# A dilated causal convolution with a gated output on one core: staging copies and input loads tied to TensorE's place in the plan, other DMA durations in the planner, and two items of a unit exchanged

## The chip, the cores and the metric

The kernel runs on one core of a Trainium2 chip. The metric is device time in microseconds (us), the median over runs of the same program. The kernel before took 342.98 us (median of 3 runs, 342.66 to 343.67).

## What is computed

`x` is 2 x 16000 x 144, `w` is 15 x 144 x 288 and `w_o` is 144 x 144, all bf16. Every time step gets the sum over 15 taps, two steps apart and looking back, of a row of `x` times a 144 x 288 matrix; the two halves of the 288 results go through tanh and sigmoid, are multiplied, and the product is projected by `w_o`:

```python
xp = jnp.pad(x, ((0, 0), (pad, 0), (0, 0)))
h = jnp.einsum('btc,cd->btd', xp[:, pad:pad + T, :], w[0])
for i in range(1, K):
    off = pad - i * dil
    h = h + jnp.einsum('btc,cd->btd', xp[:, off:off + T, :], w[i])
f = h[..., :D].copy()
g = h[..., D:].copy()
z = jnp.tanh(f) * _sigmoid(g)
return z @ w_o
```

## The kernel before

**Tiling.** The 32000 time steps are cut into 128 segments of 250, one for each partition. Step `e` of all segments together is one tile: 128 segments by 144 channels. TensorE needs the channels on the partitions, so each tile is transposed. Eight steps are an *octet* `o` (0 to 30), two octets are a *pair* `m` (octets 2m+1 and 2m+2). The 144 channels are split: 128 of them go into the tiles `XA`, the other 16, of eight taps side by side, into the tiles `XB`.

**Staging of a pair.** A load brings 16 steps into `Xr` (two buffers; L476). For each octet VectorE copies the 128 channels into the contiguous buffer `STA` (L634), and a DMA transpose turns that into `XA` (L636). VectorE also packs the 16 channels into `XBc` (`compact_chunk`, L533); ScalarE copies from there, in two halves per octet, into `STB` (L653), and a DMA transpose makes `XB` of it (L655). `STA` and `STB` have two buffers each, so a copy must wait until the transpose of the octet before the last has landed. `XA` has 11 slots, `XB` 7. The function `stage(m)` adds all this to the plan for a pair. `prepare(m)` adds VectorE's differences of such tiles (L672: `V`, `DU`, `DD`, `BE`, `BF`, and `GX`, `GU`, `GV`, `GD` for a pair).

**The arithmetic of a unit.** The 15 taps are not run as 15 products per step: sums of weights (`WC`, `WS`, `WT`, `WV`, `WD`) and differences of tiles give eight outputs with fewer products. A *unit* is one parity of a pair and makes eight output steps; there are 30. Its items, in the order of the string `PATTERN`, are groups of matmuls of 128x128 weights with 288 columns (L726). `S0`, `X0a`, `X1a` and `Y0a` each run two matmuls into one bank of a pair of PSUM banks, and ScalarE copies the bank to its neighbour (L890); `S1`, `X0b`, `X1b`, `Y0b` then add to both. ScalarE moves `X` results to `UX` (L959) and `S1`'s to a second pair (L917). VectorE combines: `VE`'s and `VF`'s results plus `UX` (L1011, three per unit, into the memory of `Xp`; L1032, one), and these plus `Y` (L1023, three). The last items `D11`, `D00`, `D10`, `D01` end in tanh and sigmoid on ScalarE (L747, L750; `TS`) and a product on VectorE (L755; `Z`). A DMA transposes `Z` to `ZT` (L814), TensorE multiplies by `w_o` (L831), ScalarE copies the result to `OS` (L839), and a DMA stores it (L850). In the string, a `+` means that the item belongs to the unit after the current one; `O` marks a place for a group of `w_o` matmuls.

**The order of the work.** Nothing of this order is written out for the other engines. Each operation is added to a graph with its reads, writes, a duration and a priority, and a list scheduler (`_Graph.run`) plays the program with those durations: each engine takes the operation that can start first, TensorE's main items in the order in which they were added. What comes out is a fixed sequence for each of TensorE, ScalarE, VectorE, GpSimd and SyncE (which issues nearly all DMAs). On the chip, each engine runs its sequence strictly in order; waits are semaphores of true dependencies. The argument `soft` names operations whose planned start must come first; it shapes the sequence and is no wait on the chip. Before, `prepare`'s steps are spread over two units, twelve per pair, each `soft` on TensorE's latest operation at that place (the list `gate`); `stage`'s operations are added at once for the whole pair and carry no `soft`, so the scheduler puts them as early as buffers and engines allow. A DMA's planned end is its issue, plus its bytes at 280 GB/s, one DMA after the other, plus `DMA_LAT` (2.3 us).

Of the kernel before, what the change touches and what calls it, by code (L numbers as in the profile page):

```python
# [9 lines left out]
F32 = mybir.dt.float32  # L10

NP = 128
DMA_LAT = 2.3
DMA_RATE = 280e3
MM = 0.1227
TAIL = {"pe": 0.165, "act": 0.095, "dve": 0.088, "pool": 0.1, "sp": 0.0}
# [56 lines left out]
class _Graph:  # L73
# [58 lines left out]
    def run(self, hint):  # L132
# [18 lines left out]
        dma_free = 0.0  # L151
# [40 lines left out]
        while n < len(self.ops):  # L192
# [34 lines left out]
            free[op.eng] = st + op.dur  # L227
            if op.dma:
                t0 = max(dma_free, st + op.dur)
                dma_free = t0 + op.nbytes / DMA_RATE  # L230
                op.end = dma_free + DMA_LAT
            else:
                op.end = st + op.dur + TAIL[op.eng]
            ai[0] += 1 if op.alloc and not op.floating else 0
# [93 lines left out]
def _conv_wavenet_kernel(nc, x, w, w_o, out):  # L328
# [19 lines left out]
    NPAIR = NOCT // 2  # L348
# [7 lines left out]
    NX = 2  # L356
# [11 lines left out]
    KF = 6  # L368
    LAG = 2
    SPREAD = 12  # L370
    PATTERN = "Y0a O2+ X0a+ O1+ Y0b X0b+ D11 D00 X1a+ S0+ D10 Y01 S1+ X1b+ D01 VE+ O0+ VF+"

    with contextlib.ExitStack() as st:
        def sb(name, shape, dt):
# [38 lines left out]

        g = _Graph()

        XpF = Xp[:].rearrange("p e d -> p (e d)").bitcast(F32)

        def bank(b):
# [211 lines left out]
        def load_xa(o):  # L630
            s, q = aslot(o), o % NST
            ci = chunk_of(8 * o)
            i0 = 8 * o - CH[ci][0]
            g.add("dve", lambda v: v.tensor_copy(STA[:, q, :, :], Xr[:, ci % NX, i0:i0 + 8, 0:DA]),  # L634
                  r=[("Xr", ci % NX)], w=[("STA", q)], dur=0.335, prio=2)
            g.add("sp", lambda e: e.dma_start_transpose(XA[:, s, :, :], STA[:, q, :, :].rearrange("p a b -> p (a b)")),  # L636
                  r=[("STA", q)], w=[("XA", s)], dur=1.3, dma="xa", nbytes=8 * 128 * 128 * 2)

        def load_xb(o):
            s, q = bslot(o), o % NST  # L640
            e0 = E0 + 8 * o
            ck = set()
            for e in range(e0 - 28, e0 + 8):
                if e >= EP:
                    ck.add(("XBc", chunk_of(e - E0)))
                else:
                    ck.update(hk5 + ["XBcz"])
            m4 = (e0 + 2) // 4

            for h in range(2):  # L650
                def cp(v, h=h):
                    src = bass.AP(XBc[:].tensor, (MB - 1 - m4 - h) * DB, [[4 * MB * DB, NP], [MB * DB, 4], [1, 128]])
                    return v.activation(STB[:, q, 4 * h:4 * h + 4, :], src, ACT.Copy)  # L653
                g.add("act", cp, r=sorted(ck, key=str), w=[("STB", q, h)], dur=0.5, prio=2)
            g.add("sp", lambda e: e.dma_start_transpose(XB[:, s, :, :], STB[:, q, :, :].rearrange("p a b -> p (a b)")),  # L655
                  r=[("STB", q, 0), ("STB", q, 1)], w=[("XB", s)], dur=1.3, dma="xb", nbytes=8 * 128 * 128 * 2)

# [1 line left out]
            return [("XB", bslot(o))]  # L659

        TR = 128
        gate = []

        def ap(t, off, dims):
            full = t[:].tensor
# [487 lines left out]
            b_diffs(o)  # L1153

        def stage(m):

            if m >= NPAIR:
                return
            for o in (2 * m + 1, 2 * m + 2):
                fetch(o)  # L1160
                if o > 2:
                    load_xa(o)
                    while nd[0] < len(CH) and CH[nd[0]][0] <= 8 * o:
                        compact_chunk(nd[0])
                        nd[0] += 1
                    load_xb(o)

        def prepare(m):
            o0, o1 = 2 * m + 1, 2 * m + 2
# [13 lines left out]
        reach = max(o for _, o in pattern)  # L1183
        todo = [(-1, 2, 1), (0, 0, 2), (0, 1, 2), (0, 2, 2)]
        done_d = {}
        stage(1)
        for f in prepare(0):
            f()
        todo_p = []
        for t in range(-reach, NUN):  # L1190
            if t % 2 and t >= -1:
                stage((t + 1) // 2 + 2)
                todo_p = prepare((t + 3) // 2)
                step = 0
            for name, off in pattern:
                while todo_p and step * SPREAD >= (12 - len(todo_p)) * 2 * len(pattern):
                    gate[:] = [op for op in g.ops[-40:] if op.eng == "pe"][-1:]
                    todo_p.pop(0)()
                    gate[:] = []
                step += 1  # L1200
                if name[0] == "O":
                    for _ in range(2 if t >= NUN - 3 else 1):
                        if t >= 0 and todo and todo[0][2] <= t:
                            project(*todo.pop(0)[:2])
                    continue
                u = t + off
                if not 0 <= u < NUN:
                    continue
                if name[0] == "G":
                    if (u, int(name[1]), int(name[2])) in late:  # L1210
                        late.pop((u, int(name[1]), int(name[2])))()
                    continue
                ITEMS[name](u)
                if name[0] == "D":
                    done_d[u] = done_d.get(u, 0) + 1
                    m, r, o0, o1 = octs(u)
                    if done_d[u] == 4 and r == 1 and u < NUN - 1:
                        for o in (o0, o1):
                            ship(o, range(8))
                            todo += [(o, gi, t + LAG) for gi in range(3)]  # L1220
                    elif done_d[u] == 4 and u == NUN - 2:
                        for o in (o0, o1):
                            ship(o, (0, 2, 4, 6))
# [98 lines left out]
```

## Time and profile before

| what | value |
|---|---|
| time, median of 3 runs | 342.98 us |
| the profiled execution's own time | 342.79 us |
| its span, first to last instruction | 340.8 us |
| mean granted TensorE clock | 0.997 |
| TensorE matmul busy | 327.4 us (96%) |
| VectorE busy | 303.3 us (89%) |
| ScalarE busy | 258.8 us (76%) |
| GpSimd busy | 17.5 us (5%) |

The profile is of one execution. Engines are called PE (matmul), PEld (weight load, beside PE), DVE (VectorE), ACT (ScalarE), POOL (GpSimd) and SP (SyncE; SPq is its queue). A row of the timeline gives the start of a run of like instructions from the span's start, how long it lasted, engine, line, operation, tiles written and read, shape and count; in brackets stands the engine's idle time ahead of it and what ended it. A matmul's recorded end is modelled and lies beyond the start of the next one. Rows of the stage table give, for each stretch, each engine's busy time with its count of instructions, the granted clock and the DMA engines' busy share.

### The profile page before, as it was taken

The page shows a single profiled execution, that of the slowest core. Times are in us where ns is not written, and L with a number is a line of the kernel's source. Part 1 is how long each engine was busy: PE and PEld are TensorE (multiplying, and loading weights), DVE is VectorE, ACT ScalarE, POOL GpSimd, SP SyncE. Part 2 cuts the span into 40 slices and gives each one's busy share as a digit, 9 for nine tenths or more (in the row PEclk, how much of TensorE's full clock was granted, in tenths as well). Part 3 has the DMA queues.
Part 4 walks back from the last instruction along what each step waited for, and adds up shares of the span by engine and source line. Part 5 has one row for each costly group of instructions (what it writes and reads, how often), then busy time and mean ns, then how long its engine had stood idle before and what let it go on. Part 6 is the DMA issues. An engine that isn't in the chain of part 4 may idle for free.

```text
span 340.8 us, 7123 instructions
## 1 busy us (share of the span) xinstructions
PE 327.4 (96%) x2736; PEld 246.3 (72%) x2736; DVE 303.3 (89%) x662; ACT 258.8 (76%) x626; POOL 17.5 (5%) x30
## 2 busy tenths in 40 slices
PE   7899899799999999999999999999999999999996
PEld 6777576476777777777777777777777777777773
DVE  2999889799989999999999999998998989895672
ACT  3238477888888978788797878888887777778764
POOL 8650000000000000000000000000000000000000
PEclk9999999999999999999999999999999999999998
DMA  8789999877657495965957496570654261231453
GB/s 214 252 133 212 237 224 197 184 160 169 120 145 151 113 188 116 203 132 143 129 144 141 109 202 132 101 148 19 145 86 105 67 87 54 61 79 37 104 106 104
DMA packets 112509, 46.46 MB, mean 136 GB/s; under 512 B 103822, under 2 KB 106303, under 8 KB 112477
## 3 DMA queue, kind: packets, MB, share of 16 engines
q1 hardware_dynamic: 111961, 45.68, 63.1%
q8 instruction: 21, 0.34, 0.4%
q0 software_dynamic: 512, 0.33, 0.4%
q14 instruction: 11, 0.09, 0.1%
q10 hardware_dynamic: 4, 0.01, 0.0%
HBM read 11.82 MB, written 9.22 MB: 62 GB/s over the span
## 4 chain that ended last, share of the span: by engine, by line
PE 80%; DMA 8%; ACT 5%; DVE 5%; issue 1%; SPq 1%
PE PS L726 70%; PE PS L831 7%; DMA XB<-STB 6%; ACT STB L653 2%; DMA Xp<-in_x_dram 1%; DVE Xp L1011 1%; ACT UX L959 1%; ACT TS L747 1%; ACT TS L750 1%; DVE PS L1023 1%; DVE WC L614 1%; ACT PS L890 0%; DVE Z L755 0%; SPq L476 0%; PE PS L781 0%
## 5 line engine op out<-in xcount | busy, mean ns | idle before, releaser
L1011 DVE TENSOR_TENSOR Xp<-PS,UX 128x576 f32<-128x576 f32 x90 | 65.2, 752 | 13.8 <-PE PS L726 13.0
L1023 DVE TENSOR_TENSOR PS<-PS,Xp 128x576 f32<-128x576 f32 x90 | 68.4, 760 | 2.7 <-PE PS L726 1.1
L726 PE MATMUL PS<-WA,GD 128*128 128x288 bf16 x360 | 69.9, 286 | 0.3 <-DVE PS L1023 0.3
L890 ACT ACTIVATE PS<-PS 128x288 f32<-128x288 f32 x120 | 45.7, 406 | 22.7 <-PE PS L726 22.7
L747 ACT ACTIVATE TS<-PS 128x288 f16<-128x288 f32 x125 | 51.8, 414 | 11.1 <-PE PS L726 9.0
L750 ACT ACTIVATE TS<-PS 128x288 f16<-128x288 f32 x125 | 51.6, 413 | 0.0
L959 ACT ACTIVATE UX<-PS 128x576 f32<-128x576 f32 x60 | 39.0, 650 | 15.9 <-PE PS L726 13.7
L653 ACT ACTIVATE STB<-XBc 128x512 bf16<-128x512 bf16 x60 | 36.3, 633 | 16.3 <-DMA XB<-STB 11.3
L726 PE MATMUL PS<-WS,GU 128*128 128x288 bf16 x210 | 44.1, 286 | 0.0
L839 ACT ACTIVATE OS<-PS 128x432 bf16<-128x432 f32 (+1 forms) x88 | 42.4, 488 | 0.8
L755 DVE TENSOR_TENSOR Z<-TS 128x288 bf16<-128x288 f16 x125 | 37.6, 301 | 5.9 <-ACT TS L750 5.7
L831 PE MATMUL PS<-WOR,ZT 128*128 128x144 bf16 (+1 forms) x322 | 42.3, 253 | 0.2 <-ACT TS L750 0.2
L726 PEld LDWEIGHTS PS<-WA,GD 128*128 128x128 bf16 x360 | 34.6, 98 | 10.5 <-DVE PS L1023 1.9
L726 PE MATMUL PS<-WB,XB 128*128 128x288 bf16 x140 | 37.6, 286 | 0.0
L726 PE MATMUL PS<-WB,BF 128*128 128x288 bf16 x120 | 34.3, 286 | 0.0
L726 PE MATMUL PS<-WB,BE 128*128 128x288 bf16 x120 | 34.3, 286 | 0.0
L831 PEld LDWEIGHTS PS<-WOR,ZT 128*128 128x128 bf16 x322 | 27.9, 98 | 6.7 <-ACT OS L839 0.6
L726 PE MATMUL PS<-WD,DD 128*128 128x288 bf16 x180 | 31.9, 286 | 0.2 <-ACT PS L890 0.2
L726 PE MATMUL PS<-WA,DD 128*128 128x288 bf16 x180 | 30.8, 287 | 0.1
L726 PE MATMUL PS<-WC,V 128*128 128x288 bf16 x180 | 30.6, 286 | 0.0
L726 PE MATMUL PS<-WT,DU 128*128 128x288 bf16 x120 | 24.8, 288 | 2.4 <-DVE Xp L1011 1.6
L726 PEld LDWEIGHTS PS<-WS,GU 128*128 128x128 bf16 x210 | 20.3, 98 | 5.7 <-ACT PS L890 0.4
(89 smaller groups left out, 517.7 us busy)
## 6 DMA issues: line engine op xcount, KB each, us to landing
Xr<-in_x_dram SPq DMA_DIRECT2D x15, 576.0 KB, 4.0
out_dram<-OS SPq DMA_DIRECT2D x29, 288.0 KB, 2.4
WA<-in_w_dram SPq DMA_DIRECT2D x3, 288.0 KB, 5.7
ZT<-Z SPq DMA_TRANSPOSE x32, 3.6
Xp<-in_x_dram SPq DMA_DIRECT2D x2, 252.0 KB, 5.7
XA<-STA SPq DMA_TRANSPOSE x30, 3.4
XB<-STB SPq DMA_TRANSPOSE x30, 3.3
Xp<-in_x_dram SPq DMA_DIRECT2D x1, 441.0 KB, 3.7
```

The costliest lines, as they stand in the source:

```text
L614: g.add(eng, lambda v: v.tensor_tensor(dst(), a(), b(), ALU.add), r=r, w=wk, dur=dur)
L653: return v.activation(STB[:, q, 4 * h:4 * h + 4, :], src, ACT.Copy)
L726: return lambda t: t.matmul(bank(bk.b), lhsT=lhs(), rhs=rhs(), start=start, stop=True, skip_group_check=True)
L747: return a.activation(TS[:, s, 0, :, :], both(bk, 0, D), ACT.Tanh)
L750: return a.activation(TS[:, s, 1, :, :], both(bk, D, D), ACT.Sigmoid)
L755: return v.tensor_tensor(dst, TS[:, s, 0, :, :], TS[:, s, 1, :, :], ALU.mult)
L831: return t.matmul(PS[:, c0:c0 + n * D], lhsT=ZT[:, zt, blk, :], rhs=WOR[:, wi:wi + n, :].rearrange("p a b -> p (a b)"), start=first, stop= ...
L839: return e.tensor_copy(dst, src) if eng == "dve" else e.activation(dst, src, ACT.Copy)
L890: g.add("act", lambda e: e.activation(bank(bk.b + 1), bank(bk.b), ACT.Copy), w=[bk], dur=t_act(N2), prio=0)
L959: g.add("act", lambda e: e.activation(UX[:, k, u % NU, :, :], both(X, 0, N2), ACT.Copy), r=[X], w=[("UX", k, u % NU)], frees=[X], dur=t_ac ...
L1011: g.add("dve", lambda v, k=k, wi=wi, vb=vb, us=us: v.tensor_tensor(wslot(wi), both(vb, 0, N2), UX[:, k, us, :, :], ALU.add), r=[vb, ("UX", ...
L1023: return v.tensor_tensor(both(d, 0, N2), src, wslot(wi), ALU.add)
```

## The change

Three things. First, `stage` no longer adds a pair's staging at once: it returns seven steps (two loads, the packing, two `XA` octets, two `XB` octets), which the main loop releases at even distances over part of two units (`SPREAS`), and the copies into `STA` and `STB` carry `soft` on the TensorE operation that was added last before them. `gate` is now set once for each place of the pattern, from main items alone. Second, the planner's DMA model: a transpose moves its bytes at 168 GB/s and then takes 0.6 us, the first loads of `x` and the weights keep 2.3 us, every other DMA takes 1.3 us after its bytes. Third, `S0` and `X1a` change places in `PATTERN`.

```diff
             if op.dma:
                 t0 = max(dma_free, st + op.dur)
-                dma_free = t0 + op.nbytes / DMA_RATE
-                op.end = dma_free + DMA_LAT
+                turn = op.dma in ("xa", "xb", "zt")
+                dma_free = t0 + op.nbytes / (DMA_RATE * (0.6 if turn else 1.0))
+                op.end = dma_free + (0.6 if turn else 2.3 if op.dma in ("xp", "wa", "wb") else 1.3)
...
-    PATTERN = "Y0a O2+ X0a+ O1+ Y0b X0b+ D11 D00 X1a+ S0+ D10 Y01 S1+ X1b+ D01 VE+ O0+ VF+"
+    SPREAS = 10
+    PATTERN = "Y0a O2+ X0a+ O1+ Y0b X0b+ D11 D00 S0+ X1a+ D10 Y01 S1+ X1b+ D01 VE+ O0+ VF+"
...
-                  r=[("Xr", ci % NX)], w=[("STA", q)], dur=0.335, prio=2)
+                  r=[("Xr", ci % NX)], w=[("STA", q)], dur=0.335, prio=2, soft=gate[:1])
...
-                g.add("act", cp, r=sorted(ck, key=str), w=[("STB", q, h)], dur=0.5, prio=2)
+                g.add("act", cp, r=sorted(ck, key=str), w=[("STB", q, h)], dur=0.5, prio=2, soft=gate[:1])
...
         def stage(m):
-
             if m >= NPAIR:
-                return
-            for o in (2 * m + 1, 2 * m + 2):
-                fetch(o)
-                if o > 2:
-                    load_xa(o)
-                    while nd[0] < len(CH) and CH[nd[0]][0] <= 8 * o:
-                        compact_chunk(nd[0])
-                        nd[0] += 1
-                    load_xb(o)
+                return []
+            o0, o1 = 2 * m + 1, 2 * m + 2
+
+            def pack():
+                while nd[0] < len(CH) and CH[nd[0]][0] <= 8 * o1:
+                    compact_chunk(nd[0])
+                    nd[0] += 1
+            return [lambda: fetch(o0), lambda: fetch(o1), pack, lambda: load_xa(o0), lambda: load_xa(o1), lambda: load_xb(o0), lambda: load_xb(o1)]
...
             if t % 2 and t >= -1:
-                stage((t + 1) // 2 + 2)
-                todo_p = prepare((t + 3) // 2)
+                todo_p, n_p, todo_s, n_s = prepare((t + 3) // 2), 12, stage((t + 5) // 2), 7
                 step = 0
             for name, off in pattern:
-                while todo_p and step * SPREAD >= (12 - len(todo_p)) * 2 * len(pattern):
-                    gate[:] = [op for op in g.ops[-40:] if op.eng == "pe"][-1:]
+                gate[:] = [op for op in g.ops[-60:] if op.eng == "pe" and not op.floating][-1:]
+                while todo_p and step * SPREAD >= (n_p - len(todo_p)) * 2 * len(pattern):
                     todo_p.pop(0)()
-                    gate[:] = []
+                while todo_s and step * SPREAS >= (n_s - len(todo_s)) * 2 * len(pattern):
+                    todo_s.pop(0)()
+                gate[:] = []
```

The sequences of the engines that come out differ as follows; after the change the line numbers are one or two higher (L653 becomes L655, L634 L636, L890 L891, L1011 L1012).

ScalarE near the start, from the copies for octet 4 on, before: `STB` rows are the staging copies, `UX` and `PS<-PS` belong to unit 0, `TS` is tanh and sigmoid.

```order
L653 ACTIVATE STB<-XBc 128x512 x2
L959 ACTIVATE UX<-PS 128x576
L890 ACTIVATE PS<-PS 128x288 x2
L653 ACTIVATE STB<-XBc 128x512 x2
L959 ACTIVATE UX<-PS 128x576
L917 ACTIVATE PS<-PS 128x2x288
L653 ACTIVATE STB<-XBc 128x512 x4
L747 ACTIVATE TS<-PS 128x288
L750 ACTIVATE TS<-PS 128x288
L890 ACTIVATE PS<-PS 128x288 x2
```

The same place after:

```order
L655 ACTIVATE STB<-XBc 128x512 x2
L960 ACTIVATE UX<-PS 128x576
L891 ACTIVATE PS<-PS 128x288 x2
L960 ACTIVATE UX<-PS 128x576
L918 ACTIVATE PS<-PS 128x2x288
L655 ACTIVATE STB<-XBc 128x512 x2
L891 ACTIVATE PS<-PS 128x288
L748 ACTIVATE TS<-PS 128x288
L751 ACTIVATE TS<-PS 128x288
L655 ACTIVATE STB<-XBc 128x512
L891 ACTIVATE PS<-PS 128x288
L655 ACTIVATE STB<-XBc 128x512
```

Before, the copies of octets 5, 6 and 7 stand ahead of this tanh; after, only octet 5's do, octet 6's stand behind it, and octet 7's come some thirty instructions later.

ScalarE in the middle of the run, around the start of a unit that has staging, before:

```order
L839 ACTIVATE OS<-PS 128x432
L653 ACTIVATE STB<-XBc 128x512 x2
L959 ACTIVATE UX<-PS 128x576
L653 ACTIVATE STB<-XBc 128x512
L747 ACTIVATE TS<-PS 128x288
L750 ACTIVATE TS<-PS 128x288
L747 ACTIVATE TS<-PS 128x288
L750 ACTIVATE TS<-PS 128x288
L890 ACTIVATE PS<-PS 128x288 x2
L653 ACTIVATE STB<-XBc 128x512
```

After, the four copies of a pair stand here:

```order
L748 ACTIVATE TS<-PS 128x288
L751 ACTIVATE TS<-PS 128x288
L655 ACTIVATE STB<-XBc 128x512
L840 ACTIVATE OS<-PS 128x288
L655 ACTIVATE STB<-XBc 128x512
L891 ACTIVATE PS<-PS 128x288
L840 ACTIVATE OS<-PS 128x432
L891 ACTIVATE PS<-PS 128x288
L840 ACTIVATE OS<-PS 128x432
L655 ACTIVATE STB<-XBc 128x512 x2
L960 ACTIVATE UX<-PS 128x576
```

All four moved ahead of the `UX` copy of `X0b`; none is left among the tanh and sigmoid rows of the unit.

VectorE in the middle of the run, the second half of a unit with staging, before:

```order
L672 TENSOR_TENSOR V<-XA 128x1024
L672 TENSOR_TENSOR DU<-XA 128x512
L755 TENSOR_TENSOR Z<-TS 128x2x144
L634 COPY STA<-Xr 128x1024 x2
L755 TENSOR_TENSOR Z<-TS 128x2x144
L672 TENSOR_TENSOR GX<-XA 128x512
L1023 TENSOR_TENSOR PS<-PS,Xp 128x2x288
L755 TENSOR_TENSOR Z<-TS 128x2x144
L672 TENSOR_TENSOR GU<-DU 128x1024
L1011 TENSOR_TENSOR Xp<-PS,UX 128x576
```

After:

```order
L535 COPY XBc<-Xr 128x4x4x16
L673 TENSOR_TENSOR V<-XA 128x1024
L756 TENSOR_TENSOR Z<-TS 128x2x144
L673 TENSOR_TENSOR DU<-XA 128x512
L756 TENSOR_TENSOR Z<-TS 128x2x144
L636 COPY STA<-Xr 128x1024
L1024 TENSOR_TENSOR PS<-PS,Xp 128x2x288
L756 TENSOR_TENSOR Z<-TS 128x2x144
L673 TENSOR_TENSOR GX<-XA 128x512
L673 TENSOR_TENSOR GU<-DU 128x1024
L636 COPY STA<-Xr 128x1024
L1012 TENSOR_TENSOR Xp<-PS,UX 128x576
```

The two `STA` copies of a pair stand apart, the second directly ahead of the first combine of the next `VE`; the packing into `XBc` is in this unit, where before it stood in the other. TensorE's main items keep their order but for the exchange of `S0` (`WT,XA`) and `X1a` (`WT,DU`).

6 lines of the change are left out of this document (3 added, 3 removed).

## The prediction

> **What bounds the kernel now.** I read the page, then busy time in three stretches, cut where `S1` starts in unit 0 (31.76 us), unit 3 (68.78) and unit 27 (301.64). The first holds three units and the rest of the direct products for the first outputs, the second 24 units, the third the end.
>
> ```profile
> span 340.8 us, 7123 instructions
> PE 327.4 (96%) x2736; PEld 246.3 (72%) x2736; DVE 303.3 (89%) x662; ACT 258.8 (76%) x626; POOL 17.5 (5%) x30
> ...
> PE 80%; DMA 8%; ACT 5%; DVE 5%; issue 1%; SPq 1%
> ```
> ```profile
> 31.76:68.78 37.02, 32.39 (x255) 23.28 (x252) 32.50 (x74) 26.15 (x63) 0.00 (x0) 1.00 0.97 203
> 68.78:301.64 232.86, 231.62 (x1897) 173.26 (x1897) 221.74 (x473) 192.37 (x471) 0.00 (x0) 1.00 0.61 125
> 301.64:340.80 39.16, 35.62 (x294) 26.12 (x293) 23.96 (x49) 26.33 (x66) 0.00 (x0) 0.97 0.34 84
> ```
>
> TensorE is on the chain that ended last for 80% of the span, and busy for 96%. Its rows in the first stretch, and in two units of the second, give its pace and its waits.
>
> ```profile
> 25.76 1.63 PE L726 MATMUL PS<-WB,XB 128*128 128x288 bf16 x12
> 27.23 0.41 PE L726 MATMUL PS<-WT,DU 128*128 128x288 bf16 x2
> ...
> 39.21 0.42 PE L726 MATMUL PS<-WV,V 128*128 128x288 bf16 x2 [0.92 <-DVE Xp L1011]
> ...
> 41.34 0.42 PE L726 MATMUL PS<-WT,DU 128*128 128x288 bf16 x2 [0.73 <-ACT TS L750]
> ...
> 44.96 0.42 PE L726 MATMUL PS<-WA,GD 128*128 128x288 bf16 x2 [0.32 <-DVE PS L1023]
> ...
> 51.79 0.42 PE L726 MATMUL PS<-WT,DU 128*128 128x288 bf16 x2 [0.42 <-DVE Xp L1011]
> ...
> 61.27 0.42 PE L726 MATMUL PS<-WV,V 128*128 128x288 bf16 x2 [0.89 <-ACT UX L959]
> 61.87 0.55 PE L831 MATMUL PS<-WOR,ZT 128*128 128x144 bf16 x4 [0.18 <-ACT TS L750]
> 63.54 0.42 PE L726 MATMUL PS<-WT,DU 128*128 128x288 bf16 x2 [1.13 <-DVE Xp L1011]
> ```
> ```profile
> 199.99 0.53 PE L831 MATMUL PS<-WOR,ZT 128*128 128x144 bf16 x4
> 200.36 0.65 PE L726 MATMUL PS<-WD,DD 128*128 128x288 bf16 x4
> ...
> 204.52 0.41 PE L726 MATMUL PS<-WD,DD 128*128 128x288 bf16 x2
> 204.87 0.66 PE L726 MATMUL PS<-WC,GX 128*128 128x288 bf16 x4
> ...
> 208.80 0.53 PE L831 MATMUL PS<-WOR,ZT 128*128 128x144 bf16 x4
> 209.35 0.42 PE L726 MATMUL PS<-WT,DU 128*128 128x288 bf16 x2
> ...
> 213.02 0.41 PE L726 MATMUL PS<-WT,DU 128*128 128x288 bf16 x2
> 213.46 0.42 PE L726 MATMUL PS<-WT,XA 128*128 128x288 bf16 x2
> ```
>
> Twelve matmuls of 288 columns go from 25.76 to 27.23: one every 0.1225 us. Two last 0.41, so the recorded end lies 0.16 us beyond the point where the next could start: a wait in brackets is 0.16 longer for TensorE, and one under 0.16 isn't shown. A unit has 68 such matmuls (8.33 us) and three `w_o` groups, two of four (0.37 each, 199.99 to 200.36) and one of three (0.25: a matmul of 288 columns less). That is 9.32 us without a wait. The second stretch takes 232.86/24 = 9.70 per unit: 0.38 lost in each, 9.1 us in all. In the first stretch there are 252 matmuls, 11 of them in `w_o` groups: 241 x 0.1225 + 0.99 = 30.5, so 6.5 us are lost. DVE's busy time in the second stretch, 221.74 or 9.24 per unit, is the next bound, right under TensorE's 9.32.
>
> **The first stretch, term by term.** ScalarE here, and one row of VectorE:
>
> ```profile
> 33.87 0.64 ACT L917 ACTIVATE PS<-PS 128x576 f32<-128x576 f32 x1
> 37.10 1.15 ACT L653 ACTIVATE STB<-XBc 128x512 bf16<-128x512 bf16 x2 [2.59 <-DMA XB<-STB]
> 39.54 1.15 ACT L653 ACTIVATE STB<-XBc 128x512 bf16<-128x512 bf16 x2 [1.29 <-DMA XB<-STB]
> 40.60 0.39 ACT L747 ACTIVATE TS<-PS 128x288 f16<-128x288 f32 x1
> ...
> 60.04 0.63 ACT L653 ACTIVATE STB<-XBc 128x512 bf16<-128x512 bf16 x1 [1.93 <-DMA XB<-STB]
> ```
> ```profile
> 36.06 0.23 DVE L533 COPY XBc<-Xr 128x256 bf16<-128x256 bf16 x1 [1.09 <-DMA Xr<-in_x_dram]
> ```
>
> Staging copies placed too early sit at the head of ScalarE's queue and wait for the transpose that still reads their buffer; tanh, sigmoid and `UX` copies behind them wait too, and TensorE waits for these. After the change octet 6's copies stand behind the tanh of 40.60 and octet 7's far later. So:
> - 41.34 (0.73 + 0.16 = 0.89) goes; what is late next is octet 6's copy, but the transpose that it needs landed at 37.10 even now.
> - 61.27, 61.87 and 63.54 (0.89 + 0.18 + 1.13 + 3 x 0.16 = 2.68) follow from the copy at 60.04. They go, but for about 0.06 at `X0a`: 2.6.
> - 51.79 (0.58): no copy of DVE's into `STA` stands ahead of this combine any more. The rest of the chain stays; I take 0.2.
> - 39.21 (0.92 + 0.16 = 1.08): DVE's first combine stood behind the packing that waited 1.09 for its load; now the packing stands behind two combines, and one `STA` copy between them. I take half, 0.5; the bounds are 0 and 1.08.
> - 44.96 (0.48) waits for a bank and stays.
>
> Sum 4.2, and about 0.3 for three waits at `S1` (next part): 4.5. Bounds: 3.0 (39.21 and 51.79 stay, 41.34 halves) and 5.3 (all but 44.96 and the rest of 51.79).
>
> **The second stretch.** Three waits of a unit matter. At `S1` (`WC,GX`, 204.87) the two matmuls before it would have let it start at 204.77: 0.10, since ScalarE copies `X1a`'s bank first and `S0`'s second. With `S0` first, its copy runs first, earlier by the other copy (0.40 long, as at 228.51), and the 0.10 goes; `X1a`'s copy is wanted only after `S1`, 0.49 later. At 209.35 `X0a` should have started at 209.17 (0.18), at 213.46 `S0` at 213.26 (0.20): both in the unit with staging, where ScalarE's sequence is this:
>
> ```profile
> 222.27 0.41 ACT L747 ACTIVATE TS<-PS 128x288 f16<-128x288 f32 x1 [0.43 <-PE PS L726]
> ...
> 226.85 0.41 ACT L750 ACTIVATE TS<-PS 128x288 f16<-128x288 f32 x1
> 227.28 0.41 ACT L839 ACTIVATE OS<-PS 128x288 bf16<-128x288 f32 x1
> 228.51 0.40 ACT L890 ACTIVATE PS<-PS 128x288 f32<-128x288 f32 x1 [0.81 <-PE PS L726]
> ...
> 231.33 0.62 ACT L653 ACTIVATE STB<-XBc 128x512 bf16<-128x512 bf16 x1
> 231.86 0.41 ACT L747 ACTIVATE TS<-PS 128x288 f16<-128x288 f32 x1
> ```
>
> A copy holds ScalarE for 0.53 (231.33 to 231.86), a tanh row for 0.3. Ahead of a tanh it delays the release of the bank that `S0` takes: the 0.20. After the change no copy stands there. Two stand between 227.16 (end of the sigmoid row) and the `L890` copy at 228.51: 1.35 us, into which 2 x 0.53 and the `OS` copy's 0.3 just fit. The other two go ahead of `UX`, which comes some 0.3 late; 0.43 of idle time before the next tanh hides that. If a copy costs 0.1 more than here, `X0a`'s copy is late and `X0b` waits about 0.2 per pair.
>
> DVE keeps its amount of work. The best units now, near the end, where nothing is staged:
>
> ```profile
> 282.55 0.66 PE L726 MATMUL PS<-WC,GX 128*128 128x288 bf16 x4
> ...
> 292.05 0.42 PE L726 MATMUL PS<-WC,GX 128*128 128x288 bf16 x2
> ```
>
> 9.50, with the 0.10 at `S1` still in it. After the change every unit has one long difference (0.68, as at 232.19 below) between the combines that `D11` waits for; I let that cost the 0.10 again. So I take 9.50 for all 24: 24 x (9.70 - 9.50) = 4.9. Bounds: 9.47, if the difference costs 0.07 (5.6 us), and 9.63, if two thirds of the wait at `S1` are all that goes (1.6 us). DVE's 9.24 leaves room for 9.50, but little.
>
> The other DMA durations act through the sequence alone, which is counted above. The two `S1` waits of the tail go: 0.2, between 0 and 0.4.
>
> **Loads and transposes.** The staging now runs about a pair ahead instead of as far as buffers allow. What hides it:
>
> ```profile
> DMA to landing us min/median/max: 3.0/3.4/5.4
> ```
> ```profile
> 227.04 0.76 DVE L1011 TENSOR_TENSOR Xp<-PS,UX 128x576 f32<-128x576 f32 x1
> ...
> 232.19 0.68 DVE L672 TENSOR_TENSOR V<-XA 128x1024 bf16<-128x1024 bf16 x1
> ```
>
> The first row is of the transposes into `XA`. The second `STA` copy of a pair ends with its unit; the `V` that reads the tile stands 5 us into the unit after the next (as 227.04 to 232.19): 9.5 + 5 = 14.5 us for at most 5.4 and an issue behind one other. About 8 us are spare, so I cost this at nothing; on SP only the two `ZT` transposes and a store stand between, and these have all of a unit as well. `XB` is wanted later still. The trace says that early issue is what hurts: 5.8 us of ScalarE's time in the first stretch (2.59 + 1.29 + 1.93) went into waiting for early transposes. The Trainium skill, DMA: Bandwidth & Descriptors, section Rules for kernel authors, has it the other way: issue a DMA early, compute, and wait for it late. By that rule the change gives lead away, and its time would be that of the last rival.
>
> **The sum.** 342.79 (the profiled execution) - 4.5 - 4.9 - 0.2 = 333.2. That execution is 0.2 under the median, 342.98: **333.4 us**. With all bounds: 342.98 - 5.3 - 5.6 - 0.4 = 331.7, and 342.98 - 3.0 - 1.6 - 0 = 338.4.
>
> **The rivals.**
> - *The waits of a unit only change place.* `X1a` takes over `S0`'s wait for a bank, and the four copies in a row overfill ScalarE's 1.35 us, so that the second stretch stays at 9.70. For it: no slack is left in that gap, and DVE is 9.24 of 9.50. Against it: the gap fits by these rows. 342.98 - 4.5 - 0.2 = 338.3.
> - *The change doesn't do at the start what it says.* `soft` shapes the sequence alone; if the chip's transposes there take over 5.8 us, octet 5's and 6's copies still wait and TensorE with them. For it: the DMA share is 0.97. Against it: fewer transposes are then in flight. 342.98 - 4.9 - 0.2 = 337.9.
> - *Both*: about 342.8, within 0.3%, which is what a measurement of this kernel can tell from no change.
> - *Slower: the transposes land late.* `V` waits for `XA` on DVE, and with so little room there TensorE waits as long. It decides once issue and landing together take over 14.5 us; with 1 us over, in 13 pairs, it is 342.98 + 13 - 9.6 = 346.4. Against it: the longest landing is 5.4.
>
> **Chances.** Forecast 0.65, waits change place 0.20, start unchanged 0.08, both 0.03, late transposes 0.04. The first three are faster by over 0.3%: 0.93; same 0.03; slower 0.04. The range, 331.7 to 338.4, is that of the forecast's bounds and holds the first two rivals; the last two cases, and what may lie under the bounds, are left out.
>
> **What would show it.** Right: no ScalarE wait of an `STB` copy for a DMA over 0.5 us; no TensorE wait over 0.5 between 39 and 64 but for that at 44.96; units of 9.5 from `S1` to `S1`, alike with and without staging; no wait at `WC,GX`. Wrong: a new wait of `WS,GU` for `L891` (copies overfill ScalarE), `WT,DU` waiting for `L751` in every second unit (the bank wait moved to `X1a`), DVE's `V` waiting for a DMA into `XA`, or DVE idle under 1% with TensorE at 9.7 per unit (DVE is the bound). The prediction is wrong outside 331.7 to 338.4, and its mechanism is wrong if the gain lies in one stretch alone.

## The result and the profile after

The changed kernel takes 333.12 us (median of 4 runs, 332.53 to 333.94); the kernel before, in 4 runs beside it, 343.33 us (342.66 to 343.91). The ratio is 0.9705, with a 95% interval of 0.9676 to 0.9734. The forecast was 333.4. The profiled execution after took 333.25 us, its span 331.2 us.

The page of after, first its head and then the last line of its chain:

```profile
span 331.2 us, 7123 instructions
PE 323.0 (98%) x2736; PEld 249.4 (75%) x2736; DVE 302.6 (91%) x662; ACT 259.4 (78%) x626; POOL 17.2 (5%) x30
...
PE 93%; DVE 5%; ACT 1%; issue 1%; POOL 0%; POOLq 0%
```

The work is the same, to the instruction. What is new is the chain: TensorE carries 93% of it, not 80%. DMA and SyncE's queue, 9% of it before, are gone from it. Next the stage table of after, cut at the same three `S1`:

```profile
31.39:64.45 33.06, 31.96 (x259) 24.17 (x256) 30.95 (x68) 23.42 (x57) 0.00 (x0) 1.00 0.71 140
64.45:291.88 227.43, 227.43 (x1899) 174.59 (x1897) 223.55 (x479) 195.96 (x478) 0.00 (x0) 1.00 0.67 141
291.88:331.20 39.32, 35.40 (x295) 26.26 (x292) 23.96 (x49) 26.43 (x67) 0.00 (x0) 0.95 0.33 83
```

| stretch | before | after | difference | forecast |
|---|---|---|---|---|
| up to unit 0's `S1` | 31.76 | 31.39 | -0.37 | 0 |
| units 0 to 2 | 37.02 | 33.06 | -3.96 | -4.5 |
| 24 units | 232.86 (9.70 each) | 227.43 (9.48 each) | -5.43 | -4.9 |
| the end | 39.16 | 39.32 | +0.16 | -0.2 |
| sum | 340.8 | 331.2 | -9.6 | -9.6 |

The first stretch now has 256 matmuls, not 252: four direct products (0.49 us) moved into it from ahead of unit 0's `S1`. Counted by lost time, it went from 6.5 to 33.06 - 245 x 0.1225 - 0.99 = 2.06 us, a gain of 4.4. The first row then is +0.12 instead of -0.37.

TensorE's waits that the trace of after still shows in brackets between 36 and 64 us:

```profile
43.02 0.42 PE L727 MATMUL PS<-WA,GD 128*128 128x288 bf16 x2 [0.32 <-DVE PS L1024]
49.58 0.42 PE L727 MATMUL PS<-WT,DU 128*128 128x288 bf16 x2 [0.27 <-DVE Xp L1012]
59.31 0.42 PE L727 MATMUL PS<-WT,DU 128*128 128x288 bf16 x2 [0.39 <-DVE Xp L1012]
```

None is for ScalarE any more, and the first is the one at 44.96 that was to stay. ScalarE in the same place, from `S1`'s copy on:

```profile
33.49 0.64 ACT L918 ACTIVATE PS<-PS 128x576 f32<-128x576 f32 x1
34.04 1.14 ACT L655 ACTIVATE STB<-XBc 128x512 bf16<-128x512 bf16 x2
37.95 0.40 ACT L891 ACTIVATE PS<-PS 128x288 f32<-128x288 f32 x1 [2.78 <-PE PS L727]
38.26 0.41 ACT L748 ACTIVATE TS<-PS 128x288 f16<-128x288 f32 x1
38.55 0.42 ACT L751 ACTIVATE TS<-PS 128x288 f16<-128x288 f32 x1
38.84 0.64 ACT L655 ACTIVATE STB<-XBc 128x512 bf16<-128x512 bf16 x1
```

ScalarE still idles 2.78 us, but it waits for TensorE, whose next result it needs, and no longer for a transpose that TensorE does not need yet. The tanh that ran at 40.60 runs at 38.26. Idle time of ScalarE was never the cost; what stood behind it was.

A steady unit of after on TensorE, from `S1` to the next `S1`:

```profile
187.68 0.65 PE L727 MATMUL PS<-WC,GX 128*128 128x288 bf16 x4
...
191.60 0.53 PE L832 MATMUL PS<-WOR,ZT 128*128 128x144 bf16 x4
192.03 0.42 PE L727 MATMUL PS<-WT,DU 128*128 128x288 bf16 x2
...
193.75 0.29 PE L727 MATMUL PS<-WB,XB 128*128 128x288 bf16 x1
193.96 0.54 PE L727 MATMUL PS<-WA,DD 128*128 128x288 bf16 x3
...
197.16 0.65 PE L727 MATMUL PS<-WC,GX 128*128 128x288 bf16 x4
```

9.48 us, and only two places are late, both too little for a bracket: `X0a` at 192.03 by 0.06 (0.43 after a group of four, not 0.37) and `D11` at 193.96 by 0.09 (0.21 after one matmul, not 0.12). All but a few of the 24 units look like this, with and without staging.

### The profile page after: what moved, and what is told of

It is laid out like the page before. It is cut to its first block, busy times and chain, and to the rows that moved or that the text cites. A ratio compares the mean times of both kernels' runs of the same rounds, so it can differ in the third digit from the quotient of the medians.

```text
span 331.2 us, 7123 instructions
## 1 busy us (share of the span) xinstructions
PE 323.0 (98%) x2736; PEld 249.4 (75%) x2736; DVE 302.6 (91%) x662; ACT 259.4 (78%) x626; POOL 17.2 (5%) x30
## 4 chain that ended last, share of the span: by engine, by line
PE 93%; DVE 5%; ACT 1%; issue 1%; POOL 0%; POOLq 0%
PE PS L727 81%; PE PS L832 8%; DVE Xp L1012 2%; PE PS L541 1%; DVE WC L616 1%; DVE V L673 1%; DVE PS L1033 0%; PE PS L782 0%; PE PS L863 0%; PE PS L780 0%; PE PS L773 0%; DVE XA L574 0%; PE PS L772 0%; DVE PS L1024 0%; DVE Z L756 0%
## 5 line engine op out<-in xcount | busy, mean ns | idle before, releaser
L1012 DVE TENSOR_TENSOR Xp<-PS,UX 128x576 f32<-128x576 f32 x90 | 65.2, 752 | 7.0 <-PE PS L727 6.4
L748 ACT ACTIVATE TS<-PS 128x288 f16<-128x288 f32 x125 | 51.4, 411 | 14.7 <-PE PS L727 10.0
L891 ACT ACTIVATE PS<-PS 128x288 f32<-128x288 f32 x120 | 45.4, 401 | 17.5 <-PE PS L727 17.5
L751 ACT ACTIVATE TS<-PS 128x288 f16<-128x288 f32 x125 | 50.7, 405 | 0.0
L655 ACT ACTIVATE STB<-XBc 128x512 bf16<-128x512 bf16 x60 | 35.9, 630 | 10.0 <-DVE V L673 5.6
```

What stands on the lines that cost most here:

```text
L748: return a.activation(TS[:, s, 0, :, :], both(bk, 0, D), ACT.Tanh)
L751: return a.activation(TS[:, s, 1, :, :], both(bk, D, D), ACT.Sigmoid)
L891: g.add("act", lambda e: e.activation(bank(bk.b + 1), bank(bk.b), ACT.Copy), w=[bk], dur=t_act(N2), prio=0)
L1012: g.add("dve", lambda v, k=k, wi=wi, vb=vb, us=us: v.tensor_tensor(wslot(wi), both(vb, 0, N2), UX[:, k, us, :, :], ALU.add), r=[vb, ("UX", ...
```

## The experiments

The theory: copies that stand too early in ScalarE's fixed sequence cost the start and 0.38 us per pair later; the gate removes both; the swap removes the wait at `S1`; the DMA durations matter only where they move the sequence. The rivals: the durations do the work; the swap only moves a wait; a lead that is given away is paid for. The first six kernels are the other combinations of the three parts. "The gate" is itself several edits that stay together in all of them: the release in steps, the `soft` of the copies (the input loads are released in steps, but carry none), and the new way of setting `gate`, which moves `prepare`'s steps too. No run takes these apart. Each group of four or three kernels ran on one chip with runs of the kernel before among them (medians 343.68, 344.35 and 343.59 us), so ratios are what is compared between groups.

**1. The swap taken away.**
```diff
-    PATTERN = "Y0a O2+ X0a+ O1+ Y0b X0b+ D11 D00 S0+ X1a+ D10 Y01 S1+ X1b+ D01 VE+ O0+ VF+"
+    PATTERN = "Y0a O2+ X0a+ O1+ Y0b X0b+ D11 D00 X1a+ S0+ D10 Y01 S1+ X1b+ D01 VE+ O0+ VF+"
```


> The changed kernel with the old order of the string, X1a ahead of S0; the sequences of ScalarE, VectorE and SyncE are the same as after the change, so this is the swap alone, taken away. Theory: the wait at S1 comes back, 0.10 to 0.12 us in each of 24 units and 0.3 to 0.5 at the start and the end, while the rest of the gain stays: 333.1 + 2.9 = 336.0 us, units of 9.58 to 9.60. Rival (the wait at S1 was only the visible part of VectorE's pace, and the swap does nothing): 333.1, units of 9.48 with the wait at S1 taking the place of the one at D11.

Measured: 336.22 us, ratio 0.978 (0.9762 to 0.9798). `S1` in this kernel, at the start of a unit:

```profile
160.12 0.41 PE L727 MATMUL PS<-WD,DD 128*128 128x288 bf16 x2
160.46 0.66 PE L727 MATMUL PS<-WC,GX 128*128 128x288 bf16 x4
```

0.34 after two matmuls that need 0.245: the 0.10 is back, in every unit, and the units are 9.59 long. With the gate in place the swap is worth 24 x 0.11 = 2.6 us. The wait at `D11` is still 0.09 beside it, so it is a wait of its own.

**2. The gate alone** (old durations, old string):
```diff
+DMA_LAT = 2.3
...
-                turn = op.dma in ("xa", "xb", "zt")
-                dma_free = t0 + op.nbytes / (DMA_RATE * (0.6 if turn else 1.0))
-                op.end = dma_free + (0.6 if turn else 2.3 if op.dma in ("xp", "wa", "wb") else 1.3)
+                dma_free = t0 + op.nbytes / DMA_RATE
+                op.end = dma_free + DMA_LAT
...
-    PATTERN = "Y0a O2+ X0a+ O1+ Y0b X0b+ D11 D00 S0+ X1a+ D10 Y01 S1+ X1b+ D01 VE+ O0+ VF+"
+    PATTERN = "Y0a O2+ X0a+ O1+ Y0b X0b+ D11 D00 X1a+ S0+ D10 Y01 S1+ X1b+ D01 VE+ O0+ VF+"
```


> Stepwise, gated staging alone: the old DMA durations and the old order of S0 and X1a. Theory (the gating does the work, the DMA model next to nothing): 336 us, within 0.7 of the kernel that also has the new DMA model; no staging copy on ScalarE waits over 0.5 us for a transpose. Rival (the new DMA durations are what puts the copies in their right place): the waits of 1.3 to 2.6 us at the start come back, 338 to 340 us.

Measured: 336.83 us, ratio 0.9805 (0.9786 to 0.9823). As the theory has it: units of 9.59, and no staging copy that waits for a transpose from 30 us on. What the old durations leave is, above all, one wait at the start, for VectorE's combine behind a packing that waits 1.52 us for its load:

```profile
39.25 0.42 PE L727 MATMUL PS<-WV,V 128*128 128x288 bf16 x2 [1.41 <-DVE Xp L1012]
```

This is the wait at 39.21 of before, and longer. The gate doesn't remove it.

**3. The swap alone.**
```diff
-    PATTERN = "Y0a O2+ X0a+ O1+ Y0b X0b+ D11 D00 X1a+ S0+ D10 Y01 S1+ X1b+ D01 VE+ O0+ VF+"
+    PATTERN = "Y0a O2+ X0a+ O1+ Y0b X0b+ D11 D00 S0+ X1a+ D10 Y01 S1+ X1b+ D01 VE+ O0+ VF+"
```


> The kernel before with S0 ahead of X1a and nothing else. Theory: the waits at S1, 2.6 us in the trace of before, go: 343.3 - 2.6 = 340.7 us; the waits of the first stretch and the 0.38 us per staging pair at X0a and S0 stay. Rival (waits only change place: X1a takes over the bank wait): 343.3 us with a wait at X0a instead of at S1.

Measured: 341.0 us, ratio 0.992 (0.9897 to 0.9943). The total is what the theory said, and by its trace for the wrong reason. The 24 units are only 0.04 shorter, 9.66: the waits at `S1` are gone, and in nine units `X1a` now waits for its bank, 0.2 to 0.7 us, 2.6 in all. The longest of them, ScalarE's rows, then TensorE's:

```profile
172.06 0.62 ACT L653 ACTIVATE STB<-XBc 128x512 bf16<-128x512 bf16 x1
172.58 0.40 ACT L747 ACTIVATE TS<-PS 128x288 f16<-128x288 f32 x1
172.87 0.41 ACT L750 ACTIVATE TS<-PS 128x288 f16<-128x288 f32 x1
```
```profile
173.33 0.42 PE L726 MATMUL PS<-WT,DU 128*128 128x288 bf16 x2 [0.54 <-ACT TS L750]
```

A staging copy stands ahead of tanh, the sigmoid behind it frees the bank late, and the item that takes this bank, now `X1a`, waits. That is the first half of the prediction's first rival (`X1a` takes over `S0`'s wait for a bank), and it holds without the gate. Of the 2.7 us that this kernel gains, 1.4 lie before unit 3, where the sequence came out differently.

**4. The DMA durations alone.**
```diff
-DMA_LAT = 2.3
...
-                dma_free = t0 + op.nbytes / DMA_RATE
-                op.end = dma_free + DMA_LAT
+                turn = op.dma in ("xa", "xb", "zt")
+                dma_free = t0 + op.nbytes / (DMA_RATE * (0.6 if turn else 1.0))
+                op.end = dma_free + (0.6 if turn else 2.3 if op.dma in ("xp", "wa", "wb") else 1.3)
```


> The kernel before with the new DMA durations in the planner and nothing else; staging is still added for a pair at once and without a gate. Theory: only the sequences move, the copies still stand too early: 343.3 us, within 1.5 either way, with waits of staging copies for transposes of over 1 us at the start. Rival (the durations are what the change is about): 338 to 340 us and no such wait.

Measured: 342.46 us, ratio 0.9969 (0.9956 to 0.9983). Little in all, as expected, but it is the sum of two large terms. Its stage table up to unit 27:

```profile
31.64:65.51 33.87, 32.19 (x259) 23.89 (x256) 32.81 (x74) 26.46 (x63) 0.00 (x0) 1.00 1.07 209
65.51:301.12 235.61, 233.09 (x1897) 172.80 (x1896) 222.57 (x474) 192.92 (x471) 0.00 (x0) 1.00 0.62 126
```

The start is nearly as short as after the whole change (33.87 against 33.06, with the same 256 matmuls), and the 24 units are 2.75 us longer than before. At the start a copy still waits 3.25 us for a transpose, in ScalarE's rows:

```profile
37.63 0.63 ACT L653 ACTIVATE STB<-XBc 128x512 bf16<-128x512 bf16 x1 [3.25 <-DMA XB<-STB]
38.21 0.41 ACT L747 ACTIVATE TS<-PS 128x288 f16<-128x288 f32 x1
```

It costs nothing, because the tanh behind it comes at 38.21 all the same, as early as after (38.26): one copy stands ahead of it, not four. No TensorE row starts late between 31.64 and 43.29. I had taken a wait of over 1 us for the sign of a start as slow as before, and that was wrong: the wait has a price only through what is late behind it. In the steady units copies still stand ahead of tanh (at 131.25 and 132.35 us, one ahead of each of two tanh rows): units with staging take 10.24, those without 9.49.

**5. Gate and swap, old durations** (edit as in 2, without the line of the string).

> The changed kernel with the old DMA durations in the planner: gated staging and the swap. Theory (the durations act only through the sequence near the start, the rest is gate and swap): units of 9.48 as after the change, the start up to 1.2 us later, as between the two gated kernels without the swap: 333.1 + 0 to 1.2, so 333.1 to 334.3 us. Rival (the durations carry a part of the steady gain): over 335 us, with units over 9.52.

Measured: 335.57 us, ratio 0.9754 (0.9719 to 0.9789): the rival's time with the theory's units. These are those of after, 9.48. The start is some 2 us longer, where I allowed up to 1.2: unit 3's `S1` comes at 66.61, not 64.45. One copy waits for a transpose again, with a bank copy behind it and TensorE behind that:

```profile
36.82 0.63 ACT L655 ACTIVATE STB<-XBc 128x512 bf16<-128x512 bf16 x1 [2.03 <-DMA XB<-STB]
37.36 0.39 ACT L891 ACTIVATE PS<-PS 128x288 f32<-128x288 f32 x1
```
```profile
37.81 0.42 PE L727 MATMUL PS<-WS,GU 128*128 128x288 bf16 x2 [1.61 <-ACT PS L891]
```

For TensorE this wait is 1.77. As much again is lost further on, where ScalarE runs no staging copy at all (none between 38.30 and 59.63), by two waits that run 3 has too and the kernel after has not:

```profile
50.95 0.42 PE L832 MATMUL PS<-WOR,ZT 128*128 128x144 bf16 x3 [0.80 <-ACT TS L751]
...
52.04 0.42 PE L727 MATMUL PS<-WT,DU 128*128 128x288 bf16 x2 [0.67 <-ACT TS L751]
```

So the second rival (`soft` is no wait on the chip, and a copy can still come before its transpose has landed) is real with the old durations and the swap: it makes 1.77 of the 4.8 us that TensorE loses here in units 0 to 2. With the old durations and the old string (run 2) no copy waits at this place, and in the kernel after none does from unit 0 on.

**6. Durations and swap, no gate** (the edits of 3 and 4 together).

> New DMA durations and the swap, staging still added for a pair at once without a gate. Theory (copies that are not tied to TensorE stand ahead of tanh in the steady units, whatever the durations; the swap takes 0.10 off a unit): units of 9.82 - 0.10 = 9.72, start as with the durations alone: 342.5 - 2.6 = 339.9 us, within 1. Rival (durations and swap suffice, the gate is not needed): 333 to 335 us.

Measured: 341.8 us, ratio 0.9928 (0.9903 to 0.9952), at the edge of the theory's margin (0.9928 x 343.33 = 340.9), but its units are not: 9.81, not 9.72. Again the swap gives nothing in the 24 units, 9.81 against 9.82 with the durations alone: those without staging fall to 9.38, those with it are 10.28, with `X1a` waiting for its bank (3.8 us in nine units). Durations and swap don't replace the gate.

The six beside before and after. "Lost" is the time that TensorE loses in units 0 to 2, counted as in the first stretch above; units are the mean of the 24:

| gate | durations | swap | ratio | `S1` of unit 3 | lost | units |
|---|---|---|---|---|---|---|
| - | - | - | 1 | 68.78 | 6.5 | 9.70 |
| - | - | yes | 0.992 | 67.40 | 5.4 | 9.66 |
| - | yes | - | 0.9969 | 65.51 | 2.9 | 9.82 |
| - | yes | yes | 0.9928 | 64.58 | 2.7 | 9.81 |
| yes | - | - | 0.9805 | 65.78 | 4.0 | 9.59 |
| yes | - | yes | 0.9754 | 66.61 | 4.8 | 9.48 |
| yes | yes | - | 0.978 | 64.63 | 2.4 | 9.59 |
| yes | yes | yes | 0.9705 | 64.45 | 2.1 | 9.48 |

At the start the durations do most: with them TensorE loses 2.1 to 2.9 us there, without them 4.0 to 6.5. The gate takes 2.5 off alone, and 0.5 to 0.6 where the durations are new. The steady gain is the gate's: 2.8 us alone, 4.4 on top of the swap, 5.6 on top of the durations, 8.0 on top of both. The swap's 2.6 comes only behind the gate; without the gate the swap takes 0.9 us off the 24 units, or 0.2 where the durations are new.

**7. Less lead.** Staging released one unit later, at shorter distances:
```diff
-    SPREAS = 10
+    SPREAS = 14
...
-        todo_p = []
+        todo_p, todo_s, step_s = [], [], 0
...
-                todo_p, n_p, todo_s, n_s = prepare((t + 3) // 2), 12, stage((t + 5) // 2), 7
+                todo_p, n_p = prepare((t + 3) // 2), 12
                 step = 0
+            if t % 2 == 0 and t >= 0:
+                todo_s, n_s, step_s = stage((t + 4) // 2), 7, 0
...
-                while todo_s and step * SPREAS >= (n_s - len(todo_s)) * 2 * len(pattern):
+                while todo_s and step_s * SPREAS >= (n_s - len(todo_s)) * 2 * len(pattern):
...
+                step_s += 1
```


> The changed kernel with each pair's staging released one unit later, at half the distances: the first STA copy of a pair stands some 9.7 us later, the second 7.3, so the lead of 14.5 us between a staging copy and the V that reads the transposed tile falls to 5 to 7 us. Theory (late transposes cost nothing until issue and landing together take longer than the lead; landing is 3.0 to 5.6 us): VectorE waits for XA under 0.5 us in a pair, units 9.5 to 9.65 because half a GD difference (0.5 us) stands ahead of the combine: 333 to 337 us. Rival (lead matters as such, and the changed kernel already lives on the edge): V waits over 1 us in each of 13 pairs, over 345 us.

Measured: 335.99 us, ratio 0.976 (0.9724 to 0.9797). VectorE's two `STA` copies of a pair and the two `V` that read the transposed tiles:

```profile
140.59 0.42 DVE L636 COPY STA<-Xr 128x1024 bf16<-128x1024 bf16 x1
142.71 0.42 DVE L636 COPY STA<-Xr 128x1024 bf16<-128x1024 bf16 x1
...
147.53 0.69 DVE L673 TENSOR_TENSOR V<-XA 128x1024 bf16<-128x1024 bf16 x1
...
150.14 0.69 DVE L673 TENSOR_TENSOR V<-XA 128x1024 bf16<-128x1024 bf16 x1
```

From the end of the copy to the `V` it is 6.5 and 7.0 us, half of what the change leaves, and no `V` waits. Its landings, by the row of the tile `XA`, are

```profile
DMA to landing us min/median/max: 3.0/3.1/5.3
```

The loss of some 2 us against the changed kernel lies in units of 9.71, every second one: there `X0a` is 0.12 late and a `GD` group of a `Y` item 0.19 (148.95), behind combines ahead of which other VectorE work came out (`GD` at 143.71, `V` at 147.53). So 6.5 us of lead are enough here. The Trainium skill, DMA: Bandwidth & Descriptors, section Rules for kernel authors, says to issue a DMA early and to wait for it late; no run here shows a gain from more lead than that.

**8. What is left: a short difference ahead of `D11`.** Two exchanges in `prepare`:
```diff
-            return [lambda: v_first(o0), lambda: v_second(o0), lambda: v_first(o1), lambda: v_second(o1), lambda: g_diffs(m, ("GX",)),
-                    lambda: g_diffs(m, ("GU",)), lambda: v_third(o0), lambda: v_third(o1), lambda: g_diffs(m, ("GV",)), lambda: b_diffs(o0), lambda: b_diffs(o1),
+            return [lambda: v_second(o0), lambda: v_first(o0), lambda: v_first(o1), lambda: v_second(o1), lambda: g_diffs(m, ("GX",)),
+                    lambda: g_diffs(m, ("GU",)), lambda: g_diffs(m, ("GV",)), lambda: v_third(o0), lambda: v_third(o1), lambda: b_diffs(o0), lambda: b_diffs(o1),
```


> The changed kernel with two steps of the preparation exchanged in each half, so that VectorE has a difference of 128x512 (DU, GV) and no longer one of 128x1024 (V, DD) between the combines that D11 waits for; the sequences of TensorE and ScalarE are unchanged. Theory (the long difference costs 0.09 per unit at D11): 24 x 0.09 = 2.1 us and some 0.3 at the start: 330.7 to 331.1 us, units of 9.39, as the one unit of after whose difference there is short. Rival (V or GV stands later, and TensorE waits for that instead): 333 us or more, with waits at WC,V or WC,GV.

Measured: 333.27 us, ratio 0.9686 (0.965 to 0.9722): no difference to after that can be told. The wait at `D11` is gone, and others have come: units of 9.48 and 9.45. VectorE's rows of a unit pair:

```profile
141.50 1.02 DVE L673 TENSOR_TENSOR GD<-DD 128x768 bf16<-128x768 bf16 x2
142.44 0.76 DVE L1012 TENSOR_TENSOR Xp<-PS,UX 128x576 f32<-128x576 f32 x1
...
144.65 0.42 DVE L673 TENSOR_TENSOR DU<-XA 128x512 bf16<-128x512 bf16 x1
144.99 0.77 DVE L1033 TENSOR_TENSOR PS<-PS,UX 128x576 f32<-128x576 f32 x1
...
151.11 0.43 DVE L636 COPY STA<-Xr 128x1024 bf16<-128x1024 bf16 x1
151.89 0.76 DVE L1012 TENSOR_TENSOR Xp<-PS,UX 128x576 f32<-128x576 f32 x1 [0.35 <-PE PS L727]
```

The first combine at 142.44 now follows `GD` without a gap and is 0.10 late, which `X0a` waits for; in the other unit VectorE idles 0.35. The work only moved.

**9. The changed kernel again**, beside the next two.

> The changed kernel once more, on the same chip as the two kernels beside it, so that their ratios to the kernel before can be set against its own: 0.9705 as measured first, within its interval of 0.9676 to 0.9734.

Measured: 333.29 us, ratio 0.9696 (0.9667 to 0.9726), span 332.1. From unit 3 on its units repeat to 0.01 us; unit 0's `S1` came at 32.19, 0.8 later than in the first profile.

**10. The same sequence, shorter differences.** Two lines, in `v_first` and `v_third`. This kernel leaves out half of these differences, so its output is not the convolution; it shows only what their length costs:
```diff
-                tt(ap(V, 8 * q, [(4, 2), (2, 2), 2]), ap(XA, 8 * s + 2, [(-4, 2), (4, 2), 2]), ap(XA, 8 * s, [(0, 2), (4, 2), 2]),
+                tt(ap(V, 8 * q, [(4, 2 - (o > 6)), (2, 2), 2]), ap(XA, 8 * s + 2, [(-4, 2 - (o > 6)), (4, 2), 2]), ap(XA, 8 * s, [(0, 2 - (o > 6)), (4, 2), 2]),
...
-            tt(ap(DD, 8 * q, [(4, 2), (2, 2), 2]), ap(V, 8 * s + 2, [(4, 2), (8 * (p - s), 2), 2]), ap(V, 8 * s, [(4, 2), (0, 2), 2]),
+            tt(ap(DD, 8 * q, [(4, 2 - (o > 6)), (2, 2), 2]), ap(V, 8 * s + 2, [(4, 2 - (o > 6)), (8 * (p - s), 2), 2]), ap(V, 8 * s, [(4, 2 - (o > 6)), (0, 2), 2]),
```


> The changed kernel with every V difference of 128x1024 and every DD difference cut to 128x512 from octet 7 on (the other half of these differences is left out); the sequences of all engines are as after the change, but for these lengths. Theory (VectorE alone sets the wait at D11, by the long difference that stands ahead of the last combine): 24 units less some at the start x 0.09 = 2.0 us under the changed kernel, 331.1 us, units of 9.38, with only the 0.06 at X0a left, which is a chain through TensorE and one combine. Rival (the wait at D11 is set by ScalarE's UX copy or by a bank): 333.1 us, units of 9.48.

Measured: 330.55 us, ratio 0.962 (0.9589 to 0.9652). Units of 9.38, all of them. The combine that `D11` waits for, first after, then here:

```profile
191.22 1.42 DVE L1012 TENSOR_TENSOR Xp<-PS,UX 128x576 f32<-128x576 f32 x2
192.55 0.68 DVE L673 TENSOR_TENSOR DD<-V 128x1024 bf16<-128x1024 bf16 x1
193.15 0.76 DVE L1033 TENSOR_TENSOR PS<-PS,UX 128x576 f32<-128x576 f32 x1
```
```profile
189.65 1.42 DVE L1012 TENSOR_TENSOR Xp<-PS,UX 128x576 f32<-128x576 f32 x2
190.98 0.41 DVE L673 TENSOR_TENSOR DD<-V 128x512 bf16<-128x512 bf16 x1
191.32 0.76 DVE L1033 TENSOR_TENSOR PS<-PS,UX 128x576 f32<-128x576 f32 x1
```

0.60 between the combines became 0.34, and the wait of 0.09 at `D11` went; the same wait went in run 8, where a short difference stood in this place. So the long difference is its cause. What stays is the 0.06 at `X0a`.

**11. Short differences, other balance.** A list of places in place of `SPREAD`; `BE` and `BF` are released one by one:
```diff
-    SPREAD = 12
+    RELP = [0, 3, 6, 9, 11, 13, 15, 18, 22, 24, 26, 28, 30, 32]
...
-                while todo_p and step * SPREAD >= (n_p - len(todo_p)) * 2 * len(pattern):
+                while todo_p and step >= RELP[n_p - len(todo_p)]:
...
```
The list holds, in this order, `DU`, `V`, `V`, `DU`, `GX`, `GU`, `GV`, `BE`, `DD`, `DD`, `BF`, `BE`, `BF`, `GD`.

> The changed kernel with VectorE's preparation released by a list of places, so that a difference of 128x512 (DU, BE) stands between the combines that D11 waits for, as in the first try, but with GV moved to the half with spare time, where 0.35 us of VectorE was idle; a DD now stands between the last combine and the first of the Y combines. Theory (the first try failed because 0.27 us of VectorE's work went behind the D11 combine into a half that had only 0.20 idle): with the halves balanced the units are 9.38 to 9.42, 331 to 332 us. Rival (VectorE is so full that any exchange moves the wait to the next combine): 333 us or more, with a wait of WA,GD for the Y combine or of WT,DU for the first combine.

Measured: 335.73 us, ratio 0.9768 (0.9739 to 0.9798): my theory of the balance overshot. Units alternate between 9.38 and 9.83. VectorE ahead of the first combine of two units in a row:

```profile
142.10 1.02 DVE L673 TENSOR_TENSOR GD<-DD 128x768 bf16<-128x768 bf16 x2
143.65 0.76 DVE L1014 TENSOR_TENSOR Xp<-PS,UX 128x576 f32<-128x576 f32 x1 [0.53 <-PE PS L729]
...
152.91 0.42 DVE L636 COPY STA<-Xr 128x1024 bf16<-128x1024 bf16 x1
153.24 0.75 DVE L1014 TENSOR_TENSOR Xp<-PS,UX 128x576 f32<-128x576 f32 x1
```

The half with `GV` is now full: `X0a` comes 0.2 later there and `S0` behind it 0.23, while the other half has 0.53 to spare. Between runs 8 and 11 an even split may exist, with a `GV`'s 0.33 to be divided; it would bring 0.1 per unit at most, 2.4 us, and wasn't tried. No kernel that does all the work was shown to be faster than the changed one.

## Why the prediction was right, and where it was not

- **First stretch, 4.5.** Measured 4.4, from terms that were off in both directions, so the closeness is partly luck. The wait at 41.34 (0.89) went, and so did those at `S1` (0.3). The wait at 39.21 went as a whole, 1.08, not half. That is the new durations' doing: with the gate and without them it is 1.57 (run 2), and the packing's wait for its load near 36 us, from which it comes, is in all four traces with the old durations (0.81 to 1.52 us) and in none with the new. The group from 61.27 on gave 2.13, not 2.6: at 59.31 `X0a` still waits 0.55, because three combines stand behind `GU`, an `STA` copy and `DD` almost without a gap. At 51.79 0.43 stays (0.38 forecast). New is 0.29 at `D11`, at 51.52, behind a long difference, a term that the second stretch had and this one lacked. The wait at 44.96 stayed, at 43.02. The lower bound of 3.0 leaves out the 0.3 at `S1` that the upper bound has; with it, it is 3.3.
- **The reason for the first stretch.** "Staging copies placed too early sit at the head of ScalarE's queue" is borne out by the trace of after and, for one copy, by run 5; run 4 shows that such a wait can also cost nothing. Giving the whole to the gate was not right: "the other DMA durations act through the sequence alone, which is counted above" is true of the way and hides the size. Alone they take 3.2 us off the start, more than the gate alone, and put 2.75 on the rest.
- **Second stretch, 4.9.** Measured 5.43. The waits that were named at `S1` and `S0` went, but the sizes were off and made up for each other. Added up over the 24 units, by how late TensorE's rows start, 9.2 us became 3.75: at `S1` 2.1 became 0, at `S0` 1.9 became 0, at `X0a` 2.1 became 1.4, at `D11` 1.4 became 1.9, and some 0.9 at other places, which the forecast did not list, went too. So `X0a` and `S0` gave 2.6, not all of the 0.38 in each pair: 0.06 stays at `X0a` in every unit. And the long difference took back only 0.5, not 0.10 in each unit: it does cost 0.09 (run 10), but `D11` was late by as much in 16 of the 24 units before already, and is in 22 after.
- **Loads and transposes, 0.** Right. No `V` waits after, and none does at half the lead (run 7).
- **The end, -0.2.** Wrong: +0.16. The waits at `S1` went (0.2), but the part behind unit 29's `S1` grew from 19.28 to 19.67. It is 19.66 to 19.70 in the four kernels with the new durations and 19.22 to 19.46 in the four without, so it comes with the sequence that these make of the last groups. ScalarE's last copy ends as long after that `S1` as before (16.57 and 16.58 us). What is later is SyncE's last pair of stores, 0.44 us (337.45 before, 327.90 after): with the new durations the copy of a `w_o` group stands among the last ones, and its store (L851) and another (L799) directly ahead of that pair.
- **The rivals.** "The waits of a unit only change place" is what the swap does without the gate (runs 3 and 6); I had it at 0.20 for the whole change, without seeing that the gate decides it. "The change doesn't do at the start what it says" is in part what gate and swap do with the old durations (run 5). Its condition, transposes of over 5.8 us, is worked out from no row, and it isn't what decides: in run 5 the transposes into `XB` landed in 3.1 to 5.4 us, and a copy waited all the same. Neither rival holds for the three parts together. The parts alone give 0.8% (swap), 0.3% (durations) and 1.95% (gate), nearly the 2.95% of all; but that is no sign that they are independent. In the traces the swap alone gains 1.4 us before unit 3 and 0.9 in the 24 units, and behind the other two 0.2 and 2.6.
- **What would show it.** All the signs of a right forecast are in the trace but two. Between 39 and 64 a wait of over 0.5, by the count of matmul starts, stands at 59.31 (0.55). And ahead of unit 0 an `STB` copy still waits long: 5.58 us at 24.74 (in run 9 the row stands at 26.08, with 6.11 for a transpose; 4.71 at 25.09 before). No run shows whether that costs anything.

## What to carry to other kernels

Where an engine runs a fixed sequence, a copy that feeds a later stage must not stand in it before its buffer is free: the price is not the engine's idle time but the result that is late behind the copy, so read which operation follows the wait and who needs it. Parts of a change to a schedule can act on each other even where their gains seem to add up; one that moves a wait pays only when the thing that the wait falls back on has been mended too, so measure the parts alone and in pairs, and read the stages beside the total. Where two engines are within a few per cent of each other (here 9.38 and some 9.3 us per unit), two rearrangements of the second one only moved waits about (runs 8 and 11); what took time off was leaving work out (run 10).

## What the runs showed of the hardware

The transposes into `XA`, 256 KB each, landed 3.0 to 5.6 us after issue in the trace of after, at a DMA share of 0.67 to 0.71. The start depends on the execution: the same changed kernel began unit 0's `S1` at 31.39 us in one profile and 32.19 in another, while units 0 to 2 together took 33.06 and 33.14 and the steady units repeat to 0.01 us; a change of under 1 us ahead of unit 0 can't be read from one profile. A VectorE difference of 128x1024 bf16 takes 0.60 us from start to start, one of 128x512 0.34.
